# Four changes to a recurrence-and-experts kernel on one core: a first chunk in halves, another chunk order for the first expert, compaction matmuls beside the route's, and transfers that wait for their step

## The chip, the core and the metric

The kernel runs on one core of a Trainium2 chip. A core has five engines that run in parallel, each with its own instruction queue: TensorE (PE, matrix multiplication and transposes; PEld is its weight load), VectorE (DVE), ScalarE (ACT), GpSimd (POOL) and SyncE (SP). SP and POOL also start transfers between the chip's main memory and the two memories on the core, SBUF (working memory) and PSUM (where matmul results arrive). Engines wait for each other and for transfers through semaphores. The metric is the time of one execution on the device in microseconds (us); smaller is better.

## The reference

Two parts, one behind the other. The first is a gated recurrence over 4 sequences of 5056 tokens with 256 channels:

```
f = lower_bound + (1 - lower_bound) * sigmoid(f_logit)
h = f[:, t] * h + (1 - f[:, t]) * x[:, t]         # for t in range(5056); y[:, t] = h
```

The second is a mixture of 8 experts on the 20224 outputs. Each token has 8 scores (`logits = x @ w_gate`). All token-expert pairs are gone through by falling score; a token is assigned to the expert of a pair if it has none yet and the expert has fewer than 20224/8 = 2528 tokens:

```
for idx in order:
    tok, e = (int(idx) // E, int(idx) % E)
    if assigned[tok] >= 0 or counts[e] >= cap: continue
    assigned[tok] = e
    counts[e] += 1
for e in range(E):
    mask = assigned == e
    out[mask] = np.maximum(x[mask] @ w1[e], 0.0) @ w2[e]      # 256 -> 1024 -> 256
```

## The kernel before, in words

**Recurrence, about the first 157 us.** The tokens go through in 40 chunks of 4 tiles of 128 tokens (the last chunk has 2). For each chunk `load` lets SP fetch f_logit (`fl`) and x (`xl`), 512 KB each; `sig` takes the sigmoid on ACT and multiplies on POOL (on DVE for chunk 0); `fwd` transposes both on PE into `pf` and `pb`, ACT makes the gate `fg`, and DVE runs the scan into `g`; `back` multiplies back on PE into `pr`, together with the scores, and the rows are kept in `hr`; `store` lets SP write them to `hbuf` in main memory, 264 values a token. Loads run three chunks ahead.

**Route, compaction and experts.** For each expert in turn a *route* (`route`, with `search`, `assign`, `update`) finds by a search over thresholds which expert fills up next, its threshold, and its tokens; it consists of small PE matmuls into `rt` and DVE work on masks (`MK`, `O`, `K`, `X`, `TMP`), in a chain in which each needs the one before. As soon as the number of the expert is known, its row index for the weights stands in `wi`. Then a *compaction* (`compact`) turns the mask into a list of token numbers, `ids`: a scan into `RS`, matmuls of one-hot masks (`g`) with `RA` into `rt`, ACT's count (`junk`), and DVE's last step, which writes `ids` for 2 or 3 tiles of 128 tokens at a time, seven times an expert.

With `ids`, POOL gathers the rows of one chunk of up to 4 tiles from `hbuf` into `xg` (three buffers), one indirect transfer of 128 rows per tile. PE transposes a chunk into `pt` in two halves, at two steps of the chunk before (`TJ` and `T0` say which); ACT and DVE split it into `xh` and `xl`, a rounded value and its remainder.

**The steps.** The expert stage is one list, `todo`, of steps (expert, chunk, block j of 128 hidden units): 8 steps a chunk, 5 chunks of four tiles for an expert (6 for the first and the last expert, by `layout`). `first` issues the 6 matmuls of a step into `pw` (three buffers), ACT takes the positive part as `hh`, DVE the remainder `hl`; three steps later (`LAG`) `second` multiplies them with `w2s` into `py`, three matmuls a tile. After the last block of a chunk ACT copies two tiles at a time from `py` to `y` (three buffers) and POOL writes each tile to the output rows by an indirect transfer. The weights of an expert come by three indirect transfers (`r`, one buffer each) and are split in twelve pieces by ACT and DVE (`split`).

**What sets the order.** On PE, DVE and ACT the order is the order of the program. Routes, compactions and weight splits are generators (`Bg`): at each `tick`, several a step, each may go on by one piece, if the planner `Pace`, which adds up assumed durations, says that its inputs would be there (`due`) and the engine is not far behind PE. Transfers of the expert stage stand in the list `issues`; one is taken off it at the end of each step, more if the next step needs them. On POOL and SP, though, a transfer starts as soon as its own semaphores allow, in that queue's order.

```
    for i in range(len(todo) + LAG):
            first(k, c, j)
            tick()
            if j in at and nxt < len(order):
                trans(*order[nxt], at.index(j))
        if i >= LAG:
            second(*todo[i - LAG])
        issue(1 if i < len(todo) else 99)
        tick()
```

Nearly every instruction is issued through the helper `PacedEngine`, so the profile puts it on that helper's line, L100; instructions are told apart by the names of their tiles.

## Time and profile before

| | us |
|---|---|
| time, median of 3 runs (lowest, highest) | 1238.95 (1238.01, 1240.88) |
| the profiled execution's own time | 1243.49 |
| its span in the trace | 1241.7 |
| PE busy in it | 1190.7 |
| DVE busy | 770.2 |
| ACT busy | 536.0 |
| POOL busy | 454.7 |

The profiled execution's mean granted PE clock is 0.986 of full speed. The page cuts the span into 40 slices of 31 us; PE is below nine tenths only in the first slice, in the sixth and seventh (155 to 217 us, the first route, where nothing but a chain of small matmuls and DVE steps can run) and in the last. The median group of PE is `py<-w2s,hh`, 2560 matmuls of 289 ns; the groups into `pw` have 672 each of 387 to 389 ns.

How to read the rows: a row of a timeline has the start in us, the duration of one instruction in us (of several, marked x4, from first to last), the engine, the line, the operation, its result and its inputs, and in brackets how long the engine had been idle before and what ended it. A row of a table by stretches has the stretch, its length and then, for PE, PEld, DVE, ACT and POOL, the busy time with the number of instructions; behind them the mean granted clock of PE, the share of the transfer engines and the rate.

### The profile page before, as it was taken

What the parts mean: (1) busy time and instruction counts of PE and PEld (TensorE: products, weight loads), DVE (VectorE), ACT (ScalarE), POOL (GpSimd) and SP (SyncE); (2) the same over time, 40 slices, a digit from 0 to 9 for tenths busy, and PEclk for the clock granted to TensorE, in tenths of its full rate; (3) what the DMA queues carried; (4) which work ended last, traced back from release to release, by engine and by line L of the source; (5) the groups of instructions that cost most, each with busy time, mean ns of one, the idle gap of its engine ahead of it and who ended that gap; (6) DMA issues with size and microseconds to landing.
All of it is one profiled execution on the core that took longest, in us unless ns stands there. A gap on an engine that the chain in (4) does not pass through costs nothing.

```text
span 1241.7 us, 22969 instructions
## 1 busy us (share of the span) xinstructions
PE 1190.7 (96%) x9181; PEld 1072.9 (86%) x9181; DVE 770.2 (62%) x1845; ACT 536.0 (43%) x1104; POOL 454.7 (37%) x450
## 2 busy tenths in 40 slices
PE   7999977999889999999999999999999999999998
PEld 7999956888878878888888888889999999999997
DVE  6998977768757965886877776842452243222322
ACT  7888804423442443353254334453553343323322
POOL 6667503322342243342422342432342332332212
PEclk9999998999999999999999999999999999999999
DMA  9999983112121211311311311221131111110101
GB/s 352 360 355 364 344 256 100 44 39 86 53 59 37 85 57 49 101 48 40 113 41 36 103 48 39 74 80 36 51 90 65 52 51 35 53 53 25 43 17 34
DMA packets 51724, 123.12 MB, mean 99 GB/s; under 512 B 7969, under 2 KB 28193, under 8 KB 50593
## 3 DMA queue, kind: packets, MB, share of 16 engines
q0 software_dynamic: 18816, 58.87, 15.2%
q1 hardware_dynamic: 32256, 62.78, 14.5%
q8 instruction: 72, 1.18, 0.4%
q14 instruction: 36, 0.29, 0.1%
q10 hardware_dynamic: 544, 0.01, 0.0%
HBM read 79.56 MB, written 42.07 MB: 98 GB/s over the span
## 4 chain that ended last, share of the span: by engine, by line
PE 90%; DVE 5%; issue 1%; DMA 1%; ACT 1%; POOL 1%; another core or an unknown queue 0%; POOLq 0%; SPq 0%; ACTq 0%; DVEq 0%
PE py L100 38%; PE pw L100 35%; PE pr L100 5%; PE rt L100 5%; PE pb L100 3%; PE pf L100 2%; PE pt L100 2%; DVE MK L100 1%; DVE g L100 1%; DMA xl<-in_x_dram 1%; DMA xg<-hbuf,ids 0%; ACT junk L100 0%; DVE hl L100 0%; DVE CR L100 0%
## 5 line engine op out<-in xcount | busy, mean ns | idle before, releaser
L100 PE MATMUL py<-w2s,hh 128*128 128x256 f32 (+1 forms) x2560 | 492.7, 289 | 0.0
L100 ACT ACTIVATE hh<-pw 128x512 fp32r<-128x512 f32 (+3 forms) x336 | 192.1, 573 | 574.4 <-PE pw L100 435.0
L100 PEld LDWEIGHTS py<-w2s,hh 128*128 128x128 f32 (+1 forms) x2560 | 407.6, 189 | 17.9 <-issue 0.9
L100 DVE SCALAR_TENSOR_TENSOR hl<-pw,hh 128x512 fp32r<-128x512 f32 (+3 forms) x336 | 220.4, 657 | 301.4 <-ACT hh L100 277.2
L100 PE MATMUL py<-w2s,hl 128*128 128x256 f32 (+1 forms) x1280 | 363.0, 284 | 0.9 <-issue 0.8
L100 POOL DMA_INDIRECT out_dram<-y,ids x160 | 164.1, 1026 | 433.9 <-ACT y L100 396.4
L100 PE MATMUL pw<-xl,w1h 128*128 128x512 f32 (+3 forms) x672 | 260.5, 388 | 1.5 <-issue 1.2
L100 PE MATMUL pw<-xh,w1l 128*128 128x512 f32 (+3 forms) x672 | 261.2, 389 | 0.7 <-issue 0.7
L100 PE MATMUL pw<-xh,w1h 128*128 128x512 f32 (+3 forms) x672 | 260.1, 387 | 1.0 <-DVE hl L100 0.5
L100 POOL DMA_INDIRECT xg<-hbuf,ids x160 | 163.9, 1025 | 220.3 <-PE pt L100 77.7
L100 PEld LDWEIGHTS py<-w2s,hl 128*128 128x128 f32 (+1 forms) x1280 | 241.0, 188 | 0.6 <-issue 0.6
L100 PEld LDWEIGHTS pw<-xh,w1l 128*128 128x128 f32 x672 | 128.2, 191 | 23.5 <-issue 0.9
L100 PEld LDWEIGHTS pw<-xl,w1h 128*128 128x128 f32 x672 | 128.1, 191 | 14.0 <-issue 1.2
L100 PEld LDWEIGHTS pw<-xh,w1h 128*128 128x128 f32 x672 | 128.2, 191 | 13.3 <-issue 0.9
L100 POOL TENSOR_TENSOR xl<-fl,xl 128x1024 f32<-128x1024 f32 (+1 forms) x39 | 92.7, 2378 | 42.5 <-ACT fl L100 34.0
L100 DVE TENSOR_TENSOR_SCAN g<-fg,g,pb 128x512 f32<-128x512 f32 (+4 forms) x78 | 92.8, 1228 | 9.9 <-ACT fg L100 9.3
L100 ACT ACTIVATE junk<-rt,r 128x158 bf16<-128x158 f32 x158 | 62.0, 392 | 79.6 <-DVE r L100 68.5
L100 PE MATMUL pr<-iw,g 128*128 128x136 f32 x632 | 79.8, 279 | 0.0
L100 PEld LDWEIGHTS pr<-iw,g 128*128 128x128 f32 x632 | 75.9, 190 | 0.1
L100 ACT ACTIVATE fg<-pf,one,nomlb 128x512 f32<-128x512 f32 (+1 forms) x80 | 57.4, 768 | 1.9
L100 ACT ACTIVATE y<-py 128x512 f32<-128x512 f32 (+2 forms) x88 | 47.6, 558 | 20.7 <-PE py L100 11.9
L100 DVE TENSOR_TENSOR xl<-pt,xh 128x512 fp32r<-128x512 f32 (+1 forms) x80 | 54.0, 674 | 1.8 <-ACT xh L100 1.7
(172 smaller groups left out, 1185.7 us busy)
## 6 DMA issues: line engine op xcount, KB each, us to landing
hbuf<-hr SPq DMA_DIRECT2D x39, 528.0 KB, 8.8
fl<-in_f_logit_dram SPq DMA_DIRECT2D x39, 512.0 KB, 6.4
xl<-in_x_dram SPq DMA_DIRECT2D x39, 512.0 KB, 6.6
xg<-hbuf,ids POOLq DMA_INDIRECT x160
out_dram<-y,ids POOLq DMA_INDIRECT x160
r<-in_moe_w_dram,wi POOLq DMA_INDIRECT x24
hbuf<-hr SPq DMA_DIRECT2D x1, 264.0 KB, 9.1
fl<-in_f_logit_dram SPq DMA_DIRECT2D x1, 256.0 KB, 5.9
```

The lines of the kernel that those rows point to most:

```text
L100: r = f(*args, **kw)
```

## The change

Four things are changed at once.

**First chunk in halves.** A helper `halves(last, i)` gives two halves for chunks up to `last`, else the whole. Chunk 0 is loaded, passed through the sigmoid, multiplied and transposed in halves of two tiles; the multiplication is halved for chunk 1 too. Three small DVE instructions (`omlb`, `nomlb`, `identr`) are issued behind chunk 0's multiplications instead of ahead of them.

**First expert's chunks.** Their sizes, in tiles, go from 2, 4, 4, 4, 4, 2 to 2, 4, 4, 2, 4, 4. During the experts 0 and 1, the route (`main`) is held while the compaction of the next expert exists but has not written all its ids.

**Compaction matmuls beside the route's.** A compaction of expert 2 or later whose next piece is on PE waits up to 6 ticks for a tick in which the route has issued PE work.

**Transfers that wait for their step.** A transfer that is issued at the end of a step gets a dependency on the latest ACT instruction that takes `hh` out of `pw`. Transfers that a step needs at once (`upto`) and those behind the last step do not. In the last chunk each tile is copied and stored by itself.

```diff
...
     XT, FT, FG, GT, HR = {}, {}, {}, {}, {}
+    def halves(last, i):
+        return ((0, KT // 2), (KT // 2, KT)) if i <= last else ((0, KT),)
     def load(i):
...
         FT[i] = pin.tile([P, KT, D], F32, name="fl")
         XT[i] = pin.tile([P, KT, D], F32, name="xl")
-        for dst, src in ((FT[i], fr), (XT[i], xr)):
-            nc.sync.dma_start(dst[:np_].rearrange("p n d -> p (n d)"),
-                              src[t0 * P:(t0 + n) * P].rearrange("(p n) d -> p (n d)", n=KT))
+        for a, b in halves(0, i):
+            for dst, src in ((FT[i], fr), (XT[i], xr)):
+                rows = src[t0 * P:(t0 + n) * P].rearrange("(p n) d -> p (n d)", n=KT)
+                nc.sync.dma_start(dst[:np_].rearrange("p n d -> p (n d)")[:, a * D:b * D], rows[:, a * D:b * D])
...
     nc.scalar.dma_start(wg, w_gate.rearrange("(h p) e -> p h e", p=P))
     omlb = consts.tile([P, 2], F32, name="omlb")
-    nc.vector.tensor_scalar(omlb, lbc, -1.0, 1.0, op0=OP.mult, op1=OP.add)
     nomlb = consts.tile([P, 2], F32, name="nomlb")
-    nc.vector.tensor_scalar(nomlb, lbc, 1.0, -1.0, op0=OP.mult, op1=OP.add)
     ident_r = consts.tile([P, P], F32R, name="identr")
-    nc.vector.tensor_copy(ident_r, ident)
     iw = consts.tile([P, 2 * (P + E)], F32, name="iw")
...
     def sig(i):
         np_ = chunks[i][2]
-        nc.scalar.activation(FT[i][:np_], FT[i][:np_], AF.Sigmoid, scale=-1.0)
-        (nc.gpsimd if i else nc.vector).tensor_mul(XT[i][:np_], FT[i][:np_], XT[i][:np_])
+        for a, b in halves(0, i):
+            nc.scalar.activation(FT[i][:np_, a:b], FT[i][:np_, a:b], AF.Sigmoid, scale=-1.0)
+        for a, b in halves(1, i):
+            (nc.gpsimd if i else nc.vector).tensor_mul(XT[i][:np_, a:b], FT[i][:np_, a:b], XT[i][:np_, a:b])
...
         pb = [ppt.tile([P, 512], F32, name="pb") for h in range(2)]
-        for src, dst in ((FT[i], pf), (XT[i], pb)):
+        for src, dst, ks in [(*sd, range(a, b)) for a, b in halves(0, i) for sd in ((FT[i], pf), (XT[i], pb))]:
             for h in range(2):
                 by_k = dst[h][:, :w].rearrange("d (p k) -> d k p", k=KT)
-                for k in range(KT):
+                for k in ks:
                     nc.tensor.transpose(by_k[:, k], src[:np_, k, h * P:(h + 1) * P], ident[:np_, :np_])
...
     sig(0)
+    nc.vector.tensor_scalar(omlb, lbc, -1.0, 1.0, op0=OP.mult, op1=OP.add)
+    nc.vector.tensor_scalar(nomlb, lbc, 1.0, -1.0, op0=OP.mult, op1=OP.add)
+    nc.vector.tensor_copy(ident_r, ident)
     nc.vector.tensor_copy(iw[:, :P], ident)
...
     def layout(k):
-        ns = [2, 4, 4, 4, 4, 2] if k == 0 else [4, 4, 4, 4, 2, 2] if k == E - 1 else [4] * 5
+        ns = [2, 4, 4, 2, 4, 4] if k == 0 else [4, 4, 4, 4, 2, 2] if k == E - 1 else [4] * 5
         assert sum(ns) == NB
...
     WI, IDS, RAW, WS, XG, XS, HS, PY, SC = {}, {}, {}, {}, {}, {}, {}, {}, []
-    WAITW, WAITS, SLACK = 30, 8, 2000.0
+    WAITW, WAITS, SLACK, PAT = 30, 8, 2000.0, 6
...
     issues = []
-    def issue(n=1, upto=None):
+    gate = []
+    SYNC = mybir.DependencyInfo(mybir.DependencyClass.Sync, mybir.DependencyReason.DATA)
+    def issue(n=1, upto=None, paced=False):
         st = None
...
         for _ in range(min(n, len(issues))):
             st = issues.pop(0)[1]()
+            if paced and gate:
+                tc.add_manual_dep(st.ins, gate[-1].ins.name, SYNC, reason="one transfer per step")
         return st
...
         hh = hp.tile([P, 512], F32R, name="hh")
         hl = hp.tile([P, 512], F32R, name="hl")
-        up = post("ACT", (ps,), lambda: nc.scalar.activation(hh[:, :w], ps[:, :w], AF.Relu))
+        def evacuate():
+            gate.append(nc.scalar.activation(hh[:, :w], ps[:, :w], AF.Relu))
+        up = post("ACT", (ps,), evacuate)
         post("DVE", (hh,), lambda: v.scalar_tensor_tensor(hl[:, :w], ps[:, :w], 0.0, hh[:, :w].bitcast(F32),
...
                 nc.tensor.matmul(py, x, w, start=(j == 0 and i == 0 and q % 2 == 0),
                                  stop=(j == FB - 1 and i == 2), skip_group_check=True)
-            if j == FB - 1 and q % 2 == 1:
+            alone = (k, c) == order[-1]
+            if j == FB - 1 and alone:
+                if q % 2 == 0:
+                    PY["y"] = yp.tile([P, 2, D], F32, name="y")
+                nc.scalar.activation(PY["y"][:n, q % 2], py, AF.Copy)
+                issues.append((("s", 999), store(k, c, q, n, PY["y"])))
+                issue(99)
+            elif j == FB - 1 and q % 2 == 1:
                 turn = len(SC) // 2 + sum(what[0] == "s" for what, _ in issues) // 2
...
     class Bg:
-        def __init__(self, gen, apart=0):
+        def __init__(self, gen, apart=0, patience=0):
+            self.patience = self.idle = patience
             self.gen, self.apart, self.wait, self.done, self.need = gen, apart, 0, False, ("PE",)
...
                 if not pace.due(self.need[0], self.need[1:], SLACK):
                     return
+                if self.idle and self.need[0] == "PE" and small[0] != count[0]:
+                    self.idle -= 1
+                    return
+            self.idle = self.patience
+            if self.need[0] == "PE":
+                small[0] = count[0]
             try:
...
     comp, prog = {}, {}
+    small, count = [-1], [0]
...
                 assert k == 0 or comp[k - 1].done
                 indexed()
-                comp[k] = Bg(compact((rc, rt), ohp, IDS[k], prog[k], k == 0))
+                comp[k] = Bg(compact((rc, rt), ohp, IDS[k], prog[k], k == 0), patience=PAT if k > 1 else 0)
             yield from route(k, rt, WI[k], indexed, spawn)
...
     def tick():
         nonlocal sp, wn
-        main.tick()
+        count[0] += 1
+        if k > 1 or k + 1 not in comp or have(k + 1, "ids", sum(CHUNKS[k + 1][1])):
+            main.tick()
         flush()
...
         if i >= LAG:
             second(*todo[i - LAG])
-        issue(1 if i < len(todo) else 99)
+        issue(1 if i < len(todo) else 99, paced=i < len(todo))
         tick()
...
```

Three places of the program show the moves. First VectorE's queue between expert 1's compaction and its first ids. `RS` is the compaction's first scan, `ids` its first result, 54 rows further on before; here are the last rows of them. `M`, `K`, `KH`, `KL`, `MK` and `PRE` belong to expert 2's route, `hl`, `w2s` and `w1l` to expert 0's steps and the weights.

```order
L100 TENSOR_TENSOR K_160<-K_160,M_151 128x160
L100 COPY K_165<-K_160 128x160
L100 TENSOR_SCALAR KH<-K_165 128x160
L100 TENSOR_SCALAR KL<-K_160 128x160
L100 TENSOR_TENSOR w2s<-r_4029,w2s 128x2x256
L100 SCALAR_TENSOR_TENSOR hl<-pw,hh 128x512
L100 TENSOR_TENSOR MK<-K_165,thr_118 128x1280
L100 SCALAR_TENSOR_TENSOR hl<-pw,hh 128x224
L100 TENSOR_TENSOR w2s<-r_4029,w2s 128x2x256
L100 TENSOR_TENSOR MK<-K_165,thr_118 128x1280
L100 SCALAR_TENSOR_TENSOR PRE<-thr_118,njt_115 128x128
L100 SCALAR_TENSOR_TENSOR ids<-r 128x2
```

```order
L100 SCALAR_TENSOR_TENSOR RS<-onec,MS 128x158
L100 SCALAR_TENSOR_TENSOR hl<-pw,hh 128x512
L100 TENSOR_TENSOR xl<-pt,xh 128x480
L100 TENSOR_TENSOR st<-rt,sg 128x8
L100 TENSOR_SCALAR g_4103<-IO,st 128x256
L100 CAST RA<-rt 128x160
L100 TENSOR_TENSOR RA<-cnt,RA 128x1
L100 TENSOR_TENSOR r<-sq,rt 128x2
L100 TENSOR_SCALAR r<-rt 128x2
L100 TENSOR_SCALAR g_4139<-IO,st 128x256
L100 SCALAR_TENSOR_TENSOR hl<-pw,hh 128x512
L100 SCALAR_TENSOR_TENSOR ids<-r 128x2
```

The second piece is the whole way from `RS` to `ids` now, 11 rows: none of them is the route's. Its work on expert 2 comes later, and with it that expert's `wi`: from behind the 62nd step of `todo` to behind the 66th, expert 3's from behind the 91st to behind the 101st. Expert 2 begins at the 88th step and expert 3 at the 128th.

Second TensorE's queue. `rt<-O,MK`, `rt<-CR,tot` and `rt<-fl` are the route's small matmuls, `rt<-RA,g` a compaction's; the rows before are from shortly ahead of an expert's last chunk, where the route's stand alone between the matmuls of the steps.

```order
L100 MATMUL pw<-xh,w1h 128x512
L100 MATMUL rt<-CR,tot 128x8
L100 MATMUL pw<-xl,w1h 128x512
L100 MATMUL pw<-xh,w1l 128x512
L100 MATMUL pt<-identr,xg 128x128 x3
L100 MATMUL pt<-identr,xg 128x96
L100 MATMUL py<-w2s,hh 128x256 x2
L100 MATMUL py<-w2s,hl 128x256
L100 LDWEIGHTS eighth
L100 MATMUL rt<-fl_192,eighth 128x1
```

```order
L100 MATMUL py<-w2s,hh 128x256 x2
L100 MATMUL py<-w2s,hl 128x256
L100 MATMUL pw<-xh,w1h 128x512
L100 MATMUL pw<-xl,w1h 128x512
L100 MATMUL rt<-CR,tot 128x8
L100 LDWEIGHTS g_7300
L100 MATMUL rt<-RA,g_7300 128x160
```

In the second piece the compaction's matmuls, of which the first of three is shown, stand right behind one of the route's. Counted over the program, the groups of small matmuls that stand between the large ones of the expert stage go from 217 to 198.

Third POOL's queue, at the gathers of expert 0's chunks 1 and 2 and its first stores. `Activation` among the waits is ACT's semaphore, `DMASW` that of an earlier indirect transfer, `DVE` that of the ids.

```order
L100 DMA xg<-hbuf,ids 128x264 [waits DVE_49]
L100 DMA xg<-hbuf,ids 128x264 [waits DMASW0_49]
L100 DMA xg<-hbuf,ids 128x264 [waits DMASW1_49]
L100 DMA xg<-hbuf,ids 128x264 [waits DMASW2_49,DVE_49]
L100 DMA xg<-hbuf,ids 128x264 [waits DMASW3_49]
L100 DMA xg<-hbuf,ids 128x264 [waits DMASW4_49]
L100 DMA out_dram<-y,ids 20224x256 [waits DMASW5_49,Activation_49]
L100 DMA out_dram<-y,ids 20224x256 [waits DMASW6_49]
```

```order
L100 DMA xg<-hbuf,ids 128x264 [waits Activation_49]
L100 DMA xg<-hbuf,ids 128x264 [waits DVE_49,Activation_49]
L100 DMA xg<-hbuf,ids 128x264 [waits DMASW0_49,Activation_49]
L100 DMA xg<-hbuf,ids 128x264 [waits DMASW1_49,DVE_49]
L100 DMA xg<-hbuf,ids 128x264 [waits DMASW2_49]
L100 DMA xg<-hbuf,ids 128x264 [waits DMASW3_49,Activation_49]
L100 DMA xg<-hbuf,ids 128x264 [waits DMASW4_49,Activation_49]
L100 DMA out_dram<-y,ids 20224x256 [waits DMASW5_49,Activation_49]
L100 DMA out_dram<-y,ids 20224x256 [waits DMASW6_49,Activation_49]
```

Before, the gathers wait for ids and free buffers alone. Now nearly all of them wait for ACT too, at the `hh` of successive steps. The transposes of a chunk of expert 0 or a later one stand at least three steps behind the last of its gathers' gating steps, except for four chunks, with one step: chunks 1 and 2 of expert 0 and the first ones of experts 1 and 3.

## Prediction

> **What bounds the kernel now.** I read the busy shares first, then the table by stretches, then the timeline inside each stretch where TensorE (PE) idles.
>
> ```profile
> PE 1190.7 (96%) x9181; PEld 1072.9 (86%) x9181; DVE 770.2 (62%) x1845; ACT 536.0 (43%) x1104; POOL 454.7 (37%) x450
> ```
> ```profile
> core 0: us, PE busy (x) PEld busy (x) DVE busy (x) ACT busy (x) POOL busy (x), PEclk, DMA share, GB/s
> 13.00:156.00 143.00, 141.67 (x1259) 139.60 (x1258) 133.10 (x211) 125.15 (x212) 98.25 (x77) 1.00 1.02 360
> 210.00:1235.00 1025.00, 1004.13 (x7517) 898.46 (x7516) 591.91 (x1490) 392.23 (x860) 338.43 (x333) 0.99 0.18 56
> 1235.00:1242.00 7.00, 0.65 (x6) 0.42 (x4) 0.00 (x0) 0.65 (x2) 1.88 (x2) 0.74 0.10 33
> ```
>
> PE is the bound in both large stages: 141.67 of 143.00 us in the recurrence stage, 1004.13 of 1025.00 in the expert stage. No matmul is removed, so the change can win only idle time (20.87 us in the expert stage), time at a slow clock, the price of switching between kinds of matmul, and the 7 us after the last matmuls. Where the 20.87 us lie is the main reading:
>
> ```profile
> 244.00:254.00 10.00, 8.07 (x75) 6.81 (x74) 3.68 (x15) 2.58 (x9) 5.69 (x6) 1.00 0.32 84
> 328.00:341.00 13.00, 8.76 (x86) 8.05 (x85) 4.22 (x13) 4.78 (x14) 7.79 (x8) 0.99 0.28 83
> 351.00:364.00 13.00, 8.67 (x71) 6.92 (x71) 6.36 (x22) 4.45 (x14) 7.74 (x8) 1.00 0.29 83
> 440.00:453.00 13.00, 10.63 (x87) 9.14 (x86) 7.03 (x18) 4.31 (x12) 8.01 (x8) 1.00 0.27 82
> 462.00:471.00 9.00, 7.12 (x65) 6.15 (x64) 4.63 (x17) 2.73 (x9) 5.31 (x5) 0.97 0.28 75
> 695.00:706.00 11.00, 9.83 (x81) 8.37 (x80) 9.66 (x29) 2.02 (x5) 6.72 (x7) 1.00 0.55 157
> 541.00:551.00 10.00, 10.00 (x86) 8.88 (x85) 7.58 (x26) 5.14 (x15) 3.85 (x4) 1.00 0.20 55
> 854.00:864.00 10.00, 10.00 (x66) 9.18 (x65) 2.04 (x3) 2.30 (x4) 3.82 (x4) 1.00 0.20 57
> ```
>
> In the first six stretches POOL issues five to eight indirect transfers one behind the other (the count behind POOL's time), and PE loses 1.93, 4.24, 4.33, 2.37, 1.88 and 1.17 us: 15.92 of the 20.87. In the last two POOL issues four, and PE is busy for all 10.00 us. After four of the first five losses, and within the 328 stretch's own tail, the granted clock falls:
>
> ```profile
> 255.00:259.00 4.00, 4.00 (x18) 3.29 (x18) 1.41 (x8) 1.50 (x5) 3.09 (x4) 0.57 0.21 73
> 340.00:344.00 4.00, 3.80 (x20) 3.80 (x21) 2.95 (x12) 1.71 (x6) 0.00 (x0) 0.58 0.00 0
> 364.00:368.00 4.00, 4.00 (x18) 3.52 (x18) 2.71 (x9) 1.25 (x6) 0.33 (x1) 0.57 0.00 0
> 453.00:457.00 4.00, 4.00 (x20) 3.26 (x19) 3.42 (x11) 1.72 (x7) 1.56 (x2) 0.57 0.02 6
> 470.00:474.00 4.00, 3.98 (x17) 3.59 (x18) 1.33 (x8) 2.52 (x8) 0.00 (x0) 0.57 0.01 4
> ```
>
> Each such 4 us at 0.57 costs a further 4 x 0.43 = 1.7 us. One loss has a plain cause, the first gather of expert 1:
>
> ```profile
> 329.23 0.16 DVE L100 SCALAR_TENSOR_TENSOR ids<-r 128x2 int32<-128x2 f32 x1 [0.80 <-ACT junk L100]
> ...
> 330.04 0.97 POOL L100 DMA_INDIRECT xg<-hbuf,ids  x1 [0.30 <-issue]
> ...
> 332.83 0.28 PE L100 MATMUL pt<-identr,xg 128*128 128x128 f32 x1 [0.66 <-DMA xg<-hbuf,ids]
> ...
> 335.34 0.28 PE L100 MATMUL pt<-identr,xg 128*128 128x128 f32 x1 [0.96 <-DMA xg<-hbuf,ids]
> ...
> 340.20 0.54 PE L100 MATMUL pt<-identr,xg 128*128 128x128 f32 x4 [1.63 <-issue]
> ```
>
> The token numbers (ids) come at 329.23, the gathers follow, and the transposes wait for each. It also gives the price of a landing: from the issue at 330.04 to the transpose that waited for it, 332.83, are 2.79 us. The other losses have no such cause; the reader of PE's result simply starts late, as here:
>
> ```profile
> 363.23 0.60 ACT L100 ACTIVATE hh<-pw 128x512 fp32r<-128x512 f32 x1 [6.83 <-remote]
> ```
>
> **The first chunk in halves.** I cost it at nothing. Steady work on PE begins with chunk 1, which is still loaded whole:
>
> ```profile
> 9.98 2.36 POOL L100 TENSOR_TENSOR xl<-fl,xl 128x1024 f32<-128x1024 f32 x1 [7.18 <-DMA xl<-in_x_dram]
> ...
> 12.39 0.88 PE L100 MATMUL pb<-ident,xl 128*128 128x128 f32 x6 [0.73 <-POOL xl L100]
> ```
>
> The same two megabytes have to pass before chunk 1's xl is there at 9.98. Halving POOL's 2.36 us multiplication starts nothing earlier; if transposes of the first half may start at once, up to some 0.3 us could be won, and a second fixed cost on POOL could lose as much. The three small DVE instructions that move behind the multiplications are hidden by PE's wait until 12.39; without that cover they would cost some 0.5 us.
>
> **Expert 0's chunk order, and the route held while the next compaction runs.** In the diff the route of expert 2 no longer fills DVE between expert 1's compaction and its ids (front part: 54 rows of DVE before, 11 now), and expert 0 ends on a chunk of four tiles. The ids then stand before the step that needs them, so the loss of 4.24 us and its slow clock, 1.7 us, go: -5.9 us. What is late next is the route of expert 2: its expert number moves from behind the 62nd step to behind the 66th, that of expert 3 from the 91st to the 101st, while their experts begin at the 88th and 128th. These 22 and 27 steps are the cover; without it a loss like that of 328 to 341 would come back, +5.9 us each.
>
> **Compaction matmuls beside the route's.** The price of a switch:
>
> ```profile
> 329.88 0.48 PE L100 MATMUL py<-w2s,hh 128*128 128x256 f32 x2
> 330.19 0.28 PE L100 MATMUL py<-w2s,hl 128*128 128x256 f32 x1
> 330.31 0.39 PE L100 MATMUL py<-w2s,hh 128*128 128x256 f32 x2
> 330.54 0.29 PE L100 MATMUL py<-w2s,hl 128*128 128x256 f32 x1
> ```
>
> The pair right behind route matmuls takes 330.19 - 329.88 = 0.31 us to the next row, the undisturbed one 0.23: a switch costs 0.08 us. In the order of the program 217 groups of small matmuls between the experts' become 198: 19 x 0.08 = 1.5 us, -1.5. Ends: 0, if waiting costs elsewhere what it saves, and twice that, if the first small matmul pays too.
>
> **Transfers that wait for their step.** Each of the gathers, stores and weight loads now waits until ACT has taken the result of its step's first matmuls, so from the third chunk on POOL issues one per step. A step of four tiles lasts about 3 us, a transfer on POOL about 1 us: runs of five to eight, and with them the five other losses, should not form. Their idle time is 1.93 + 4.33 + 2.37 + 1.88 + 1.17 = 11.7 us and the four slow clocks 4 x 1.7 = 6.9, together 18.6. Ends: 0, if the runs only stand beside the losses, and 18.6. Every one of six long runs has a loss and neither run of four, so I take a value near the upper end, -16.
>
> The SBUF — State Buffer page of the Trainium skill, section "SBUF: two separate sides", speaks against this: compute engines and DMA reach the memory by different ports, and PE and ACT never wait for anyone there. By that rule the 16 would be 0; the six stretches do not look like it, though they do not show what the engines wait for.
>
> The added wait has a price where a gather is issued just ahead of its transposes. The waiting transfer holds up all that stands behind it on POOL's queue: stores (three y buffers wait for them), the next gathers, the weights. In the program's order all but four gathers have at least three steps between their last transfer and the transposes. The four, with one step, are chunks 1 and 2 of expert 0 and the first of experts 1 and 3:
>
> ```profile
> 211.38 0.39 ACT L100 ACTIVATE hh<-pw 128x256 fp32r<-128x256 f32 x1 [1.32 <-issue]
> ...
> 224.95 0.60 ACT L100 ACTIVATE hh<-pw 128x512 fp32r<-128x512 f32 x1 [1.51 <-PE pw L100]
> ...
> 230.25 0.60 ACT L100 ACTIVATE hh<-pw 128x512 fp32r<-128x512 f32 x1 [2.11 <-PE pw L100]
> ```
> ```profile
> 213.48 0.46 PE L100 MATMUL pt<-identr,xg 128*128 128x128 f32 x4
> ...
> 226.86 0.46 PE L100 MATMUL pt<-identr,xg 128*128 128x128 f32 x4
> ...
> 232.87 0.46 PE L100 MATMUL pt<-identr,xg 128*128 128x128 f32 x4
> ```
>
> Chunk 1: activation 0.39 + landing 2.79 - (213.48 - 211.38) = 1.1 us late. Chunk 2: 0.60 + 2.79 - (226.86 - 224.95) = 1.5. The other two, by the distance in full steps: 0.60 + 2.79 - (232.87 - 230.25) = 0.8 each. Sum: +4.2 us. Weight loads come up to three steps later too, with ACT's splitting instruction waiting and the next hh behind it; PE has three pw buffers, two steps or some 6 us of cover, so I count nothing.
>
> **The tail.**
>
> ```profile
> 1235.01 0.29 PE L100 MATMUL py<-w2s,hl 128*128 128x256 f32 x1
> ...
> 1235.69 0.65 ACT L100 ACTIVATE y<-py 128x256 f32<-128x256 f32 x2 [2.50 <-PE py L100]
> 1236.35 0.97 POOL L100 DMA_INDIRECT out_dram<-y,ids  x1 [6.59 <-ACT y L100]
> ```
>
> The last two tiles are now evacuated one by one. The first is complete at 1235.30; half of 0.65 later its store can start, at 1235.65 instead of 1236.35, and the second store follows at the same distance: -0.7 us.
>
> **Sum.** -5.9 - 16 - 1.5 + 4.2 - 0.7 = -19.9 us. The profiled execution took 1243.49 us (span 1241.7 and 1.8 around it), so 1223.6 in its terms. The median of the runs is 1238.95, 4.54 less; taken off that it is 1219.0. If those 4.54 us were losses of this kind that only a profiled execution has, a run gains 4.5 less, 1223.5. I predict 1219.
>
> **The rivals.**
> First, the runs of transfers are not the cause: the losses stay, wherever they fall. For it: rows such as that of 363.23 name no transfer, and runs of four cost nothing. Against it: all six long runs. Time: 1238.95 - 5.9 - 1.5 + 4.2 - 0.7 = 1235.0. The rule of the SBUF page is this rival.
>
> Second, the four late gathers bring slow clocks: 4 x 1.7 = 6.8 us more, 1225.8. For it: the stretch 462 to 471 lost only 1.88 us and 470 to 474 is at 0.57. Against it: 695 to 706 lost 1.17, at 1.00 throughout. The page TensorE: Matmul & The Clock Gate of the Trainium skill, section "What's actually happening", has the clock halved after an idle window of about 3.4 us; by that rule waits of 0.8 to 1.5 us would bring none, and the time would stay at 1219. The row of 1.88 us shows that less than a whole window of idle time is enough.
>
> Third, slower: gathers are late as a rule. Every chunk of eight steps carries about eight transfers, one per step, and weights come on top; if the queue falls behind, a gather is issued in the step before its transposes and PE waits 0.8 us each time, at the transposes ahead of each of the 41 later chunks. It decides once the runs bring nothing and some nine more than the four are late: 4.0 us is gained by then, 9 x 0.8 = 7 lost, past 0.2%. With 21 late it is 1235.0 + 17 x 0.8 = 1248.6. Against it: the distance of three or more steps, 8 us, for all others.
>
> **How the numbers follow.** Chances: forecast 0.62, with its own range 1211 to 1224 (the runs' upper end 18.6, twice the switches, and no late gather give 1211); runs not the cause 0.18; slow clocks 0.12; late as a rule 0.08. The range that holds 8 in 10 reaches from 1210 to 1236, so that the first rival's value lies inside. About 0.2%, 2.5 us, is what a measurement of this kernel can tell from no change. Faster by more: 0.62 + 0.12 + two thirds of the first rival = 0.85, taken as 0.84; slower by more 0.09; between them 0.07.
>
> **What would show it.** In the profile of the changed kernel POOL should show no run of five transfers after some 230 us, PE should be busy for all but a few us of the expert stage, and the granted clock 0.57 should be gone there. The transposes of expert 1's first chunk should wait under 1 us; those of expert 0's second and third chunk 1 to 1.5 us. Steady work should still begin at about 12.4 us. The last store should follow the last matmul 0.7 us sooner. The prediction is wrong if single, spaced transfers still leave ACT waiting several us for finished matmuls, or if POOL's waits on hh push gathers behind their transposes in ordinary steps.

## The result, and the profile after

The changed kernel takes 1220.24 us (median of 4 runs, 1218.31 to 1220.82), the kernel before 1238.59 beside it: a ratio of 0.9838 with a 95% interval of 0.9823 to 0.9854, 18.35 us less. The forecast was 1219 in a range of 1210 to 1236. The profiled execution took 1220.07 us (span 1218.3), so this time it stands at the median and not 4.54 us above it.

The table by stretches of the changed kernel, for the places where the kernel before lost its time, and two others:

```profile
13.00:156.00 143.00, 141.15 (x1254) 138.96 (x1252) 133.22 (x213) 124.68 (x211) 97.53 (x77) 1.00 1.02 360
210.00:1212.00 1002.00, 994.82 (x7523) 894.45 (x7522) 593.65 (x1490) 392.86 (x860) 338.61 (x336) 1.00 0.19 57
...
244.00:260.00 16.00, 16.00 (x138) 14.11 (x138) 10.06 (x37) 7.38 (x23) 3.88 (x4) 1.00 0.13 35
328.00:341.00 13.00, 13.00 (x91) 12.09 (x90) 12.00 (x19) 5.23 (x13) 4.15 (x5) 1.00 0.18 51
351.00:364.00 13.00, 13.00 (x119) 11.55 (x118) 8.89 (x26) 3.96 (x11) 4.29 (x5) 1.00 0.16 43
440.00:453.00 13.00, 13.00 (x95) 11.69 (x91) 11.63 (x24) 4.85 (x12) 3.92 (x4) 1.00 0.15 46
402.00:412.50 10.50, 10.50 (x76) 9.32 (x74) 6.11 (x19) 3.10 (x6) 7.21 (x7) 1.00 0.69 217
609.00:618.00 9.00, 8.91 (x73) 7.23 (x71) 6.39 (x19) 2.44 (x6) 6.35 (x6) 1.00 0.27 79
...
217.40:220.70 3.30, 3.30 (x18) 3.06 (x16) 1.96 (x6) 1.16 (x3) 0.00 (x0) 0.50 0.00 0
```

In four stretches that held losses POOL now issues four or five transfers and PE is busy throughout. PE's idle time in the expert stage falls from 20.87 us to 1002.00 - 994.82 = 7.18, and of the five half-clock stretches behind losses none is left; a new one stands at 217 to 221. Two runs of seven and six transfers are left, at 402 and 609 us, where the prediction had none; they still make a reader late, the `hh` at their ends by 2.0 and 2.6 us, but cost PE nothing to speak of:

```profile
412.28 0.60 ACT L100 ACTIVATE hh<-pw 128x512 fp32r<-128x512 f32 x1 [4.19 <-remote]
...
617.76 1.09 ACT L100 ACTIVATE hh<-pw 128x512 fp32r<-128x512 f32 x2 [5.49 <-remote]
```

The text ahead of the prediction says that PE falls below nine tenths only at the start, in the first route and at the end. The page of before has it below also in the slices from 310 to 372 us, where two of the losses stand.

What is late now are the gathers that wait for a step. In the timeline:

```profile
212.22 0.39 ACT L100 ACTIVATE hh<-pw 128x256 fp32r<-128x256 f32 x1 [1.46 <-issue]
212.88 1.16 POOL L100 DMA_INDIRECT xg<-hbuf,ids  x1 [0.90 <-ACT hh L100]
216.66 0.28 PE L100 MATMUL pt<-identr,xg 128*128 128x128 f32 x1 [1.97 <-DMA xg<-hbuf,ids]
...
229.93 1.07 POOL L100 DMA_INDIRECT xg<-hbuf,ids  x1 [1.16 <-ACT hh L100]
232.79 0.45 PE L100 MATMUL pt<-identr,xg 128*128 128x128 f32 x3 [1.62 <-DMA xg<-hbuf,ids]
...
320.94 0.75 PE L100 MATMUL rt<-O,SB 128*8 128x64 bf16 x20
321.88 0.94 POOL L100 DMA_INDIRECT xg<-hbuf,ids  x1 [1.07 <-ACT hh L100]
324.43 0.53 PE L100 MATMUL pt<-identr,xg 128*128 128x128 f32 x4
```

POOL's idle time ends at `ACT hh`; the gather lands 3.8 and 2.9 us later, and PE waits 1.97 and 1.62 us for it. The last three rows are expert 1's first chunk: its last gather arrives as the transposes run, with no wait that the row shows; twenty of the route's small matmuls stand ahead. The start and the end:

```profile
11.85 0.33 PE L100 MATMUL pb<-ident,xl 128*128 128x128 f32 x1 [0.51 <-POOL xl L100]
...
1212.67 0.48 PE L100 MATMUL py<-w2s,hh 128*96 128x256 f32 x2 [0.47 <-ACT y L100]
1212.98 0.28 PE L100 MATMUL py<-w2s,hl 128*96 128x256 f32 x1
1213.31 0.38 ACT L100 ACTIVATE y<-py 96x256 f32<-96x256 f32 x1 [0.69 <-PE py L100]
1214.16 0.91 POOL L100 DMA_INDIRECT out_dram<-y,ids  x1 [0.31 <-issue]
```

Chunk 1's transposes run from 11.85 instead of 12.39 us. From the last matmul's end (1213.26) to the end of the span are 5.0 us instead of 6.1, but the last tile's matmuls wait 0.47 us until ACT has read the tile before.

### The profile page after: what moved, and what is told of

It reads as the page before. It is cut to its first block, busy times and chain, and to the rows that moved or that the text cites. A ratio compares the mean times of both kernels' runs of the same rounds, so it can differ in the third digit from the quotient of the medians.

```text
span 1218.3 us, 23154 instructions
## 1 busy us (share of the span) xinstructions
PE 1183.6 (97%) x9181; PEld 1070.2 (88%) x9181; DVE 772.0 (63%) x1846; ACT 536.3 (44%) x1105; POOL 451.1 (37%) x451
## 4 chain that ended last, share of the span: by engine, by line
PE 62%; issue 20%; POOL 10%; DVE 5%; DMA 1%; ACT 0%; POOLq 0%; another core or an unknown queue 0%; SPq 0%; ACTq 0%; DVEq 0%
PE py L100 23%; PE pw L100 22%; PE pr L100 5%; POOL out_dram L100 5%; PE rt L100 5%; POOL xg L100 5%; PE pb L100 3%; PE pf L100 2%; PE pt L100 1%; DVE g L100 1%; DVE MK L100 1%; DMA xl<-in_x_dram 0%; DMA xg<-hbuf,ids 0%; DVE CR L100 0%; DVE DM L100 0%
## 5 line engine op out<-in xcount | busy, mean ns | idle before, releaser
L100 POOL DMA_INDIRECT out_dram<-y,ids x160 | 159.7, 998 | 304.4 <-ACT hh L100 260.8
L100 PEld LDWEIGHTS pw<-xl,w1h 128*128 128x128 f32 x672 | 127.9, 190 | 12.5 <-DVE xl L100 0.4
L100 POOL TENSOR_TENSOR xl<-fl,xl 128x1024 f32<-128x1024 f32 (+2 forms) x40 | 92.9, 2323 | 41.6 <-ACT fl L100 33.9
```

What stands on the lines that cost most here:

```text
L100: r = f(*args, **kw)
```

## The experiments

The kernels were measured in several sessions, each on one chip and each with the kernel before beside them. Within a session the runs of before agree to 0.7%. Between the sessions they fall into two groups, and all that follows hangs on it: in some sessions the median of before is 1215.3 to 1215.9 us, in others, as in the result above, 1238.6 to 1241.4. I write "the 1216 group" and "the 1239 group". Ratios are to before in the same session. The expectations call the kernels by short names: no_gate is all but the waits.

| kernel | chip | before, us | this, us | ratio, 95% interval |
|---|---|---|---|---|
| waits alone | 14 | 1215.87 | 1230.39 | 1.0120 (1.0104 to 1.0137) |
| all but the waits | 14 | 1215.87 | 1207.46 | 0.9935 (0.9922 to 0.9949) |
| chunk order and held route alone | 14 | 1215.87 | 1211.27 | 0.9966 (0.9954 to 0.9978) |
| compaction beside the route alone | 14 | 1215.87 | 1213.76 | 0.9986 (0.9977 to 0.9995) |
| the changed kernel | 14 | 1215.84 | 1215.17 | 0.9986 (0.9977 to 0.9995) |
| changed, two gathers free | 14 | 1215.84 | 1209.27 | 0.9945 (0.9931 to 0.9959) |
| changed, added groups of gathers | 14 | 1215.84 | 1220.78 | 1.0038 (1.0025 to 1.0052) |
| the kernel before, for its trace | 7 | 1215.30 | 1214.68 | one run each |
| halves and tail alone | 10 | 1239.63 | 1239.19 | 0.9997 (0.9983 to 1.0012) |
| all but the waits | 10 | 1239.63 | 1227.09 | 0.9891 (0.9873 to 0.9909) |
| changed, added groups of gathers | 5 | 1241.38 | 1234.79 | 0.9951 (0.9931 to 0.9970) |
| changed, two gathers free | 5 | 1215.92 | 1210.83 | 0.9949 (0.9934 to 0.9964) |

**Waits alone.** The kernel before with this part of the change:

```diff
...
         for _ in range(min(n, len(issues))):
             st = issues.pop(0)[1]()
+            if paced and gate:
+                tc.add_manual_dep(st.ins, gate[-1].ins.name, SYNC, reason="one transfer per step")
...
-        issue(1 if i < len(todo) else 99)
+        issue(1 if i < len(todo) else 99, paced=i < len(todo))
```

> Only the fourth part without the tail: transfers wait for the hh of their step, all else as before. Theory of the runs (five or more indirect transfers behind one another on POOL hold up the engines that read PE's results): no run of five in the expert stage while PE is short of cover, and of the 18.6 us charged to them most goes; against it stand the late gathers, which cost 1.97 and 1.62 us and a slow clock of 1.7 in the changed kernel: 1225 to 1231 us. Rival (runs only stand beside the losses): only the late gathers are added, 1242 to 1245 us, and PE's waits on DVE's CR stay.

14.5 us slower, far outside both expectations. The stretches of its profile show where:

```profile
334.00:341.00 7.00, 2.33 (x20) 1.98 (x18) 1.34 (x5) 1.72 (x4) 4.84 (x5) 0.95 0.31 92
359.00:363.00 4.00, 2.15 (x16) 1.70 (x15) 2.38 (x5) 2.36 (x8) 1.97 (x2) 1.00 0.25 80
...
340.20:347.20 7.00, 6.42 (x33) 6.43 (x34) 2.47 (x9) 1.29 (x3) 1.00 (x1) 0.51 0.11 38
```

With the old chunk order expert 1's first gathers come late anyway; now they wait for steps too, PE idles 7.00 - 2.33 = 4.67 us there and 1.85 at the next chunk, and then runs at 0.51 for 7 us. No long run held up a reader in this kernel, but neither, as the next ones show, did one in any other trace of this group: so it says nothing on the runs yet.

**All but the waits.** The changed kernel with `paced` always false:

```diff
-        issue(1 if i < len(todo) else 99, paced=i < len(todo))
+        issue(1 if i < len(todo) else 99, paced=False)
```

> The changed kernel with the waits of the transfers taken out, the rest of the change kept. Theory of the runs: runs of five to eight return, with readers of PE's results that start late near their ends, 1228 to 1236 us. Rival: the gain came from the other parts, and without the late gathers the time is 1214 to 1217 us.

1207.46 us, the quickest kernel of the study and 8.4 us below before; below the rival's range too. Its trace has runs of eleven and thirteen transfers, and PE is busy through each:

```profile
245.00:260.00 15.00, 15.00 (x148) 13.61 (x147) 9.79 (x33) 5.90 (x15) 11.28 (x11) 1.00 0.30 87
311.00:329.00 18.00, 18.00 (x138) 16.06 (x137) 15.46 (x38) 10.74 (x31) 13.52 (x13) 1.00 0.31 91
```

**Chunk order and held route alone.**

```diff
-        ns = [2, 4, 4, 4, 4, 2] if k == 0 else [4, 4, 4, 4, 2, 2] if k == E - 1 else [4] * 5
+        ns = [2, 4, 4, 2, 4, 4] if k == 0 else [4, 4, 4, 4, 2, 2] if k == E - 1 else [4] * 5
...
-        main.tick()
+        if k > 1 or k + 1 not in comp or have(k + 1, "ids", sum(CHUNKS[k + 1][1])):
+            main.tick()
```

> Only expert 0's chunk order and the route held for the next compaction. By the sum of the prediction the loss at expert 1's first gather goes with its slow clock, 5.9 us: 1231 to 1235 us, with the runs and their losses still there elsewhere. Rival: the held route is what is late next, at expert 2 or 3, and PE waits there as long: 1237 to 1240 us.

4.6 us below before, with PE busy for all 13.00 us of 328 to 341 and idle 993.00 - 992.56 = 0.44 us in the whole expert stage:

```profile
328.00:341.00 13.00, 13.00 (x84) 11.86 (x84) 11.97 (x23) 2.71 (x5) 0.83 (x1) 1.00 0.08 21
210.00:1203.00 993.00, 992.56 (x7530) 893.93 (x7528) 593.15 (x1491) 393.84 (x861) 341.44 (x334) 1.00 0.19 58
```

Nothing is late next at experts 2 and 3. In this group the loss at expert 1's first gather is all that PE loses to waits, so this part takes all of it.

**Compaction beside the route alone.** The patience of 6 ticks in `Bg`, all else as before.

> Only the compactions that wait for a tick with route matmuls. By the sum 1.5 us: 1236 to 1238 us. Rival: the switches saved are not worth 0.08 us each, or what waits is late elsewhere: 1238 to 1240 us. If the theory of the runs holds, a change in when gathers start can also move a loss of 2 to 6 us in or out, whatever the switches do.

2.1 us below before by the medians; the interval of the ratio, 0.6 to 2.8 us, holds the 1.5 of the sum.

**The changed kernel again.** Unchanged, since the first four experiments stood beside a kernel before of 1216 us.

> The changed kernel unchanged, to see it beside the others. In the first four experiments the kernel before took 1215.87 us and runs of up to thirteen transfers stood beside no late reader and no idle PE; in the run of the prediction it took 1238.59. Theory of the chip (readers that start late behind long runs belong to the chip the kernel runs on): where the kernel before takes about 1216 us, the waits of the transfers can win nothing and cost the two late gathers, 1.97 and 1.62 us, with one or two slow clocks of 1.7, so no_gate's 1207.5 becomes 1212 to 1215 us; where it takes about 1238 us, 1219 to 1221 again. Rival (the waits are worth 12 to 16 us everywhere): 1190 to 1200 us where before takes 1216.

1215.17 us, 0.7 us (by the ratio 1.7) below before: the 18 us of the result are not there. With the waits it is 7.7 us slower than without, in the same group on the same chip, in another session. PE waits 2.24 and 1.59 us at the two late gathers.

**Two gathers free.** The changed kernel, but the gathers of expert 0's chunks 1 and 2 don't wait:

```diff
-            st = issues.pop(0)[1]()
-            if paced and gate:
+            what, emit = issues.pop(0)
+            free = what[0] == "g" and what[1:] in ((0, 1), (0, 2))
+            st = emit()
+            if paced and gate and not free:
```

> The changed kernel, but the gathers of expert 0's chunks 1 and 2 don't wait for a step. Theory of the late gathers: PE's waits of 1.97 and 1.62 us at their transposes go, and the slow clock behind the first: 3.6 to 7 us below the changed kernel on the same chip, wherever that is. Rival: the run of transfers that comes back at 205 to 225 us costs as much (only where long runs hold up readers), or the transposes wait for something else: within 1.5 us of the changed kernel.

5.9 us below the changed kernel in the same session, and no PE wait over 0.5 us between 210 us and the tail. The late gathers with their slow clock are thus most of what the waits cost. The same kernel ran once more, on chip 5:

> The changed kernel, but the gathers of expert 0's chunks 1 and 2 don't wait for a step, once more, since the chip may be another. Where before takes about 1239 us the changed kernel takes 1220.24: without PE's waits of 1.97 and 1.62 us and the slow clock of 1.7 behind the first 1213 to 1217 us, unless the run of transfers that comes back at 205 to 225 us holds up readers there: then 1217 to 1221. Where before takes about 1216: 1208 to 1211 us, as on chip 14.

The measurement fell into the 1216 group: 1210.83, 5.1 us below before. So it was not tried in the 1239 group, where the sum of 1220.24 and these 5.9 us, an estimate, would be 1214.

**The kernel before again.** One execution for its trace in the 1216 group (there on chip 7).

> The kernel before unchanged, for its trace where it takes less. Theory of the chip: the same runs of five to eight transfers on POOL, but no hh that starts more than 0.5 us late behind them, no slow clock behind 351, 440 and 462 us, and PE idle only at expert 1's first gather (2.5 to 4.5 us); 1214 to 1218 us where the seven experiments ran, about 1238 with late readers elsewhere. Rival (another execution merely falls otherwise, the chip being the same): late readers at some of the runs again, in other places, and a time between the two.

The same program as in the profile that the prediction read, and the same kind of runs:

```profile
245.00:260.00 15.00, 15.00 (x146) 13.52 (x144) 9.56 (x30) 5.89 (x15) 11.78 (x11) 1.00 0.31 91
324.00:335.00 11.00, 8.61 (x72) 7.93 (x71) 4.13 (x14) 4.45 (x12) 7.78 (x8) 0.84 0.29 86
340.00:356.00 16.00, 16.00 (x137) 13.60 (x136) 12.48 (x40) 8.04 (x26) 11.71 (x11) 1.00 0.30 83
426.00:437.00 11.00, 11.00 (x92) 9.58 (x91) 8.42 (x27) 6.25 (x18) 7.94 (x8) 1.00 0.26 80
```

Eight to eleven transfers in a row, and PE idles only in the second stretch, at expert 1's first gather. So the five other losses of the profile before belong to the condition of the 1239 group, not to the program alone. The readers say the same in every trace. Of the 336 `hh` of a kernel I count those behind 205 us that start more than 0.6 us after ACT is free and their six matmuls have ended. The nine traces of the 1216 group have none. In the five of the 1239 group the kernel before has 16, halves and tail alone 14, all but the waits 15, the changed kernel 2 and that with added gathers 8.

**Halves and tail alone.** The changed kernel with the other parts taken back.

> Only the first chunk in halves and the last tiles copied and stored one by one. By the sum of the prediction 0.7 us from the tail and nothing from the halves; the traces so far show steady PE work from about 11.9 us instead of 12.5 with the halves, and 5.0 instead of 6.0 us from the last matmul to the end, of which PE gives back 0.47 in a wait for y: 0.5 to 1.2 us below before. Rival (the half microsecond at the start is given back in the route's chain, whose own steps set its end): 0 to 0.6 us.

0.4 us, no change that can be told. The measurement fell into the 1239 group, and PE loses time again at all six stretches of the profile before, now on chip 10, from 0.7 to 4.8 us each; but slow clocks follow only two of them. Two of the losses:

```profile
351.00:364.00 13.00, 8.23 (x69) 6.79 (x69) 6.51 (x22) 4.60 (x14) 7.82 (x8) 0.92 0.32 90
440.00:453.00 13.00, 10.69 (x89) 9.29 (x87) 6.89 (x20) 4.46 (x12) 8.12 (x8) 1.00 0.27 83
```

**All but the waits again**, beside it.

> The changed kernel without the waits of the transfers, once more, since the chip may be another. Where before takes about 1216 us: 1206 to 1209 us again, 0.7% less than before. Where before takes about 1238 us, theory of the runs: late readers behind its long runs again, 1222 to 1236 us, so that the waits are worth 2 to 16 us there; rival (the parts that are left took the losses away): 1212 to 1217 us, below the changed kernel's 1220 also there.

1227.09 us, 12.5 below before and 6.9 above the changed kernel's 1220.24 (another session of the same group). Here the runs cost:

```profile
316.00:326.00 10.00, 9.23 (x79) 7.92 (x77) 7.22 (x21) 4.34 (x12) 5.99 (x6) 1.00 0.30 82
350.00:362.00 12.00, 10.22 (x85) 8.50 (x84) 4.54 (x16) 4.74 (x13) 6.78 (x7) 1.00 0.26 77
589.00:598.00 9.00, 7.88 (x77) 6.57 (x75) 4.71 (x16) 3.24 (x10) 5.87 (x6) 1.00 0.29 90
213.00:1221.00 1008.00, 995.62 (x7521) 895.16 (x7520) 592.69 (x1490) 393.07 (x861) 339.57 (x334) 1.00 0.18 57
```

The same program idled hardly at all on chip 14; here PE is idle 1008.00 - 995.62 = 12.38 us.

**Added groups of gathers.** The changed kernel with groups of 2, 4, 6 and 10 added gathers into `dum`, at steps where no route is left. `extra` issues one gather of 128 rows that waits for the `hh` of its step:

```diff
...
+        for kind in {278: "gg", 286: "gggg", 294: "gggggg", 302: "gggggggggg"}.get(i, ""):
+            extra(kind)
         issue(1 if i < len(todo) else 99, paced=i < len(todo))
```

> The changed kernel with 2, 4, 6 and 10 added gathers of 128 rows into a tile that nobody reads, at four steps of experts 6 and 7 where no route is left (about 1066, 1089, 1112 and 1135 us), each group behind the gathers of its chunk. With the stores that catch up behind them this makes runs of some 4, 8, 12 and over 20 transfers. Theory of the runs, on a chip where before takes about 1238 us: hh starts late by 0.6 to 4 us near the end of the runs of 8 and more, and the last one leaves PE idle for some us; 3 to 10 us more in all. On a chip where before takes about 1216: no late hh, no PE gap, within 1 us of the changed kernel. Rival (runs only stand beside the losses): within 1 us on every chip.

> The changed kernel with 2, 4, 6 and 10 added gathers at four quiet steps, once more, since the chip may be another. On chip 14 it took 1220.78 us beside 1215.17 for the changed kernel, its runs of 4, 8, 12 and 16 transfers stood beside no late hh, and only the run of 16 cost PE 2.70 us, in a wait for y. Theory of the runs on a chip where before takes about 1239 us: the run of 4 costs nothing; behind the runs of 8, 12 and 16 hh starts late by 0.6 to 4 us each, the last late start 0.8 to 1.8 us after the run's last transfer; the run of 16 leaves PE idle for over 2.70 us; 1224 to 1232 us. Rival (it takes the routes and compactions beside the run): no late hh at any of the four, since no route is left there. Where before takes about 1216 us: as on chip 14, 1217 to 1222 us.

On chip 14, 1216 group (the count behind POOL's time is the run with one or two neighbours):

```profile
1062.00:1070.00 8.00, 8.00 (x55) 7.40 (x54) 2.04 (x3) 1.77 (x3) 4.86 (x5) 1.00 0.23 70
1085.00:1098.00 13.00, 13.00 (x87) 11.90 (x86) 3.39 (x5) 3.91 (x8) 8.72 (x9) 1.00 0.27 84
1108.00:1126.00 18.00, 18.00 (x120) 16.36 (x119) 4.81 (x8) 5.88 (x10) 11.53 (x12) 1.00 0.30 88
1132.00:1150.00 18.00, 15.30 (x101) 13.72 (x101) 3.75 (x6) 4.47 (x8) 13.57 (x15) 1.00 0.33 97
```

On chip 5, 1239 group, the same four:

```profile
1068.00:1076.00 8.00, 8.00 (x53) 7.36 (x52) 2.05 (x3) 1.44 (x3) 4.85 (x5) 1.00 0.28 85
1091.00:1104.00 13.00, 13.00 (x84) 11.72 (x83) 3.12 (x5) 3.34 (x7) 8.38 (x9) 1.00 0.28 84
1114.00:1130.00 16.00, 14.49 (x92) 12.70 (x91) 3.42 (x5) 3.31 (x7) 9.54 (x10) 1.00 0.27 81
1139.00:1161.00 22.00, 14.96 (x94) 13.12 (x93) 3.46 (x5) 3.67 (x8) 14.07 (x15) 0.89 0.29 85
```

And the readers of PE's results there: hh behind the second and third run, then the fourth run with its first and last transfer (the brackets give ACT's whole idle time, of which the lateness is what lies behind the end of hh's matmuls):

```profile
1102.43 0.60 ACT L100 ACTIVATE hh<-pw 128x512 fp32r<-128x512 f32 x1 [2.37 <-PE py L100]
...
1128.48 0.60 ACT L100 ACTIVATE hh<-pw 128x512 fp32r<-128x512 f32 x1 [5.17 <-PE pt L100]
...
1139.60 0.95 POOL L100 DMA_INDIRECT dum<-hbuf,ids  x1 [2.22 <-ACT hh L100]
...
1149.53 0.60 ACT L100 ACTIVATE hh<-pw 128x512 fp32r<-128x512 f32 x1 [4.54 <-remote]
...
1155.98 0.97 POOL L100 DMA_INDIRECT out_dram<-y,ids  x1 [0.30 <-issue]
...
1159.46 0.60 ACT L100 ACTIVATE hh<-pw 128x512 fp32r<-128x512 f32 x1 [9.33 <-remote]
1160.60 0.79 PE L100 MATMUL py<-w2s,hh 128*128 128x256 f32 x2 [5.90 <-ACT y L100]
```

On chip 14 only the longest run costs, 2.70 us, and by a plain way: the stores stand behind ten added gathers, y is not free, PE waits for ACT. On chip 5 the run of four costs nothing, the run of seven makes hh 1.1 us late, that of ten 3.9 and that of fourteen 2.4 and 9.33, and PE idles 0, 0, 1.51 and 7.04 us. Of the 7.04 some 2.70 would be the wait for y alone, as on chip 14. There was no route and no compaction near, and the transfers were put there by hand: under the condition of the 1239 group long runs do hold up the readers, and among these four the longer the run, the longer. The last late start comes 1159.46 - (1155.98 + 0.97) = 2.5 us after the run's last instruction. That these were late by chance of place, the rival, is out. Both times were above what was expected: 1220.78 us is 5.6 above the changed kernel on chip 14, where at most 1 was expected, since the wait for y had been left out, and 1234.79 lies above the 1224 to 1232 of the second.

## Why the prediction was right, and where it was not

The number was met, 1220.24 us against 1219, and that is partly luck: two terms were mis-sized against each other, and the premise holds in one group of sessions alone, the one in which the forecast was made. The sum gave the waits 16 - 4.2 = 11.8 us and all the rest 8.1. In the 1239 group the waits are worth 5.8 and the rest 12.5.

**The waits** were to win 16 gross and lose 4.2. In the 1239 group the rest of the change wins 12.5 us, and the whole 18.35: the waits are worth 18.35 - 12.5 = 5.8 net (two sessions, one group). The late gathers cost 1.97 + 1.62 and a slow clock of 0.50 x 3.30 = 1.7 at 217 us, 5.3, so gross some 11. That long runs hold up the readers in this group is shown by the added groups, and that the waits prevent it by the count of late readers, 15 without them and 2 with them. The size was too high because the losses left without the waits, 12.38 us of idle time, are not those of before. A late reader costs PE only where its next matmul needs that reader. That the other parts moved the route's small matmuls away from some runs would explain the difference; no run shows it by itself.

**The reading behind the 16** was "every one of six long runs has a loss and neither run of four". The six stretches had been found by their losses. Between 210 and 1235 us of the same trace POOL issues eleven runs of five or more transfers, and at five of them, of five to seven transfers at 255, 501, 793, 804 and 924 us, PE loses 0 to 0.26 us. At one run of four, from 748.76 us, it loses 1.83:

```profile
500.00:514.00 14.00, 13.74 (x124) 12.02 (x123) 11.06 (x34) 4.43 (x9) 8.64 (x9) 1.00 0.49 162
748.00:756.00 8.00, 6.17 (x61) 5.40 (x59) 4.25 (x15) 3.09 (x9) 3.85 (x4) 1.00 0.26 68
```

The first stretch holds a run of seven and two later gathers. Its last two `hh` start 0.6 and 2.1 us late all the same, and behind the run of four `hh` is 2.0 us late. So runs make readers late, those of four sometimes too, and the count of transfers alone does not say what PE loses.

**The first rival** ("the runs of transfers are not the cause") gave 1235 and 0.18. For the 1239 group it is wrong. In the 1216 group the runs cost nothing, as it has it, and there the waits are a loss of 7.7 us and the whole change is worth 0.7. The rule that I set against my own sum, in the Trainium skill's page SBUF — State Buffer, section "SBUF: two separate sides", that PE and ACT wait for no transfer, fits the 1216 group, where runs of up to sixteen made no reader late, and not the row of 9.33 us, though what holds ACT there need not be the memory. The step that carried the forecast and doesn't hold in general is the reading above: cases picked from one execution, under one condition, and I took a coincidence with the machine's condition for a property of the program.

**Chunk order and held route**: -5.9 forecast, -4.6 measured in the 1216 group, where the loss at expert 1's first gather was 11.00 - 8.61 = 2.4 us of idle time and 0.16 x 11.00 = 1.8 of slow clock, 4.2 in all, not the 5.9 of the profile before. As forecast nothing was late next.

**Compaction beside the route**: -1.5 forecast, -0.6 to -2.8 measured, in the 1216 group. **Tail**: 0.7 forecast; the traces give 1.0 less the 0.47 that PE now waits. **Halves**: nothing forecast; steady work starts 12.39 - 11.85 = 0.54 us sooner, a little over the 0.3 that I bounded it with; together with the tail, alone, it can't be told from no change.

**The late gathers**: forecast 1.1, 1.5, 0.8 and 0.8 us, measured 1.97, 1.62, none and none. The first landed 3.8 us after its issue, not 2.79. For expert 1 I counted steps and left out the route's matmuls that stand between, 0.75 us of them in one row. **The second rival**, slow clocks at the late gathers, came true once of two. The wait of 1.62 us brought none, that of 1.97 one of 3.4 us at 0.50. It is not a matter of length alone: waits of 1.69 and 1.75 us at the same gather, in the two runs with added gathers, did bring one. The Trainium skill, TensorE: Matmul & The Clock Gate, section "What's actually happening", has a window of about 3.4 us that runs freely: the length agrees, but a wait shorter than the window was enough here. **The third rival**, gathers late as a rule, did not come in the changed kernel, but with the old chunk order gathers were late more often: PE waits for them 11.6 us in six places, and the waits alone are 14.5 us slower than before.

**The 4.54 us** between the profiled execution and the median were no constant to take off: after the change it is -0.17. In the profile's own terms the sum gave 1223.6 and 1220.07 came.

What stays open is what makes the two groups. It is not the chip as numbered: chip 5 stands in both, four minutes apart (if the number names one chip). Medians of what could differ don't: one indirect transfer on POOL takes 0.97 us in both groups, and a reader that is not held up starts 0.04 us behind PE in both. One thing in the traces does differ. The page gives the time from issue to landing of POOL's transfers in every run of the 1216 group and in none of the 1239 group; here the gathers, in the kernel before on chip 7 and in the profile that the prediction read:

```profile
xg<-hbuf,ids POOLq DMA_INDIRECT x160, 2.8
xg<-hbuf,ids POOLq DMA_INDIRECT x160
```

The reason is that the record of their landing signals, sixteen for a transfer, has holes there: the profile before holds 2688 of 5504, the changed kernel 4888, and every trace of the 1216 group over 99%. Whether what loses these records also holds up ACT and DVE, or whether the recording itself does, no run shows, and nothing was tried that could tell what sets the condition.

## What to carry to other kernels

Before a loss seen in one profile is charged to a pattern in the program, profile the unchanged kernel a second time, in another session: here a cause worth 23 us came and went with the machine. And list all places where the pattern stands, not only those with a loss. A wait added to a transfer can cost where the transfer is issued one step ahead of its use (two of four such places here) and cost nothing where it is three steps ahead, so such a rule should leave out the tight ones: freeing the gathers of two chunks won 5.9 us in the 1216 group. Of four changes at once, the other three together won in both groups (8.4 and 12.5 us), and the waits, which cure a symptom, only where the symptom was.

## What the runs showed of the hardware that I had not expected

One and the same program has two times on this hardware, 1216 and 1239 us, both steady within a session. In the longer one ACT starts late on PE's results at the end of indirect transfers that POOL issues back to back: by up to 2.0 us behind some runs of four, by 3.9 behind ten and 9.33 behind fourteen. In the shorter one up to sixteen made no reader late. Where readers are late, the trace also lacks part of the landing signals of these transfers. A gather issued by itself landed 2.9 us later in one place and 3.8 in another.
